# Local attention and a gated feed-forward layer on one core: scores of the first two blocks read straight from PSUM, and a new order of all operations

## The chip, the core and the metric

The kernel runs on one core of a Trainium2 chip. A core has five instruction queues: TensorE (PE in the profile, its weight loads PEld), VectorE (DVE), ScalarE (ACT), GpSimd (POOL) and SyncE (SP), which here issues all DMAs. Every queue executes its instructions in the order in which they stand, and waits for another engine through semaphores. TensorE writes into the eight banks of PSUM; the other engines read from there into SBUF. The metric is the device time of one execution in microseconds, the median of the runs.

## The reference, cut to what matters

```python
batch, heads, seq, D = 4, 8, 768, 64;  block, window = 32, 16;  nb = seq // block
k_sum = k.reshape(B, H, nb, block, D).max(axis=3)
v_sum = v.reshape(B, H, nb, block, D).mean(axis=3)
scores_l = scale * q @ k.T ;  mask_l = abs(i - j) < window
scores_s = scale * q @ k_sum.T + log(block)
scores_all = concat([where(mask_l, scores_l, -1e9), scores_s])
a = exp(scores_all - max(scores_all));  a = a / (sum(a) + 1e-9)
x = (a @ concat([v, v_sum])) as [3072 tokens, 512]
h = x @ w_in                       # 512 -> 2048
out = (h * cos(h)) @ w_out         # 2048 -> 512, all in float32
```

## The kernel before, in words

**Blocks and steps.** The 3072 tokens are cut into eight blocks of 384 (0 to 7, two for each of the four sequences). Attention of a block is done in four groups, one for each pair of heads, called a, b, c, d: `c0` is pair 2 of block 0. The feed-forward part is cut into 128 steps s0 to s127: a block by one of 16 slices of 128 of the 2048 hidden columns. Block 0 has s0 to s5 (hidden slices 0 to 5) and, after block 1's s6 to s21, its other ten, s22 to s31; the blocks from 2 on have 16 steps in a row. The weights of hidden slice f are w0 to w15.

**Attention of a group.** Keys and queries are loaded (L453) and turned by TensorE. The scores of a group stand in two PSUM banks, one for each head of the pair: 128 rows x 3 x 120 values each, that is 96 keys of the window and 24 block summaries for each half tile of 64 queries. For the groups of blocks 0 and 1 (the string `MASKS`) the mask is first put into the bank by TensorE: `place_masks` multiplies the identity by the float32 tile `mask` in two products, L556 for the window's columns and L559 for the summaries' columns, and `scores` (L569, L581) adds to it, with the queries already scaled. Then the two banks are copied to one SBUF tile of 128 x 6 x 120 (`scale`, which is a plain copy here, L366 on ScalarE or L368 on VectorE), VectorE takes the maximum of each row (L600), GpSimd subtracts it from the whole tile (`less_max`, L605), ScalarE takes the exponential of the whole tile in one instruction (L618), VectorE sums the rows (L621; a column of 1e-9 behind the 120 is summed too) and takes the reciprocal (L626), GpSimd multiplies by it (`normalize`, L629). TensorE turns the probabilities (`turn_p`, L638), they are copied to SBUF, and `values` (L682) multiplies them by the value rows; the result x is split into a high part `xh` and a low part `xl` (`rest`, L372). In the later blocks the scale and the mask go in with the copy from PSUM (L592).

**Values.** Value windows come by L474 and L482. The block means of the values come from their own loads, L897 for sequence 0 (products on TensorE, L905, in one bank of 512 columns) and L250 for the others, in eight pieces of 192 KB for each sequence, which GpSimd or VectorE add up (L255, L274). A piece can be loaded once its predecessor in the same buffer is added up, and the load waits for that on SP's queue. L489 spreads the means of sequence 0 to a group's value tile.

**A weight slice.** Two DMAs of about 511 KB (L387, L391) bring the packed weights; ScalarE takes them apart (`apart`, L400, `first_bits`, L406), VectorE joins the bits (`join`, L413), ScalarE or VectorE rounds to the high part (L366, L368), and VectorE or GpSimd forms the low part (`rest`, L372). Each of these is one instruction of 128 x 1024 for a slice.

**A step.** `up` (L726): 12 products of 384 columns over the four pairs c = 0 to 3, for each `wi_h` by `xh`, `wi_h` by `xl`, `wi_l` by `xh`. Then `turns` (L736, ScalarE), `residue` (L739, VectorE), `sine` (L744, ScalarE), `gate` (L748, VectorE), the high and low parts `gh` and `gl`, and the down products (L777) into three banks, which stay taken for a block's whole run: six with `gh` (`down`) and three with `gl` (`down_low`).

**What sets the order.** A hand-written string `ORDER` lists all operations of the program as words such as `a0.tk.1.0`: who (`a0` group, `s3` step, `w4` slice, `v1_2` piece 2 of sequence 1's value means), what (`l` load, `q` `k` `v` `m` loads of queries, keys, values and means, `tq` `tk` turns, `sc` scores, `z` scale, `mx` maximum, `su` less_max, `ex` exponential, `sm` sums, `iv` reciprocal, `nm` normalize, `tp` turn_p, `va` values, `xh` `xl` the parts of x, `up` `tu` `re` `si` `ga` `hi` `lo` `dh` `dl` the operations of a step), then PSUM banks or buffers as numbers, and the engine as a letter (a ScalarE, v VectorE, p GpSimd). The program is written out in that order, so each engine's queue has the order of its own words. A tile in SBUF that is reused, and a PSUM bank, makes its next writer wait for its last reader.

```python
MASKS = "11111111000000000000000000000000"
RUNS = ((0, 0, 6, "first"), (1, 0, 16, "whole"), (0, 6, 16, "last"))
```

Of the kernel before, what the change touches and what calls it, by code (L numbers as in the profile page):

```python
# [26 lines left out]
SLOTS = "6701676701267667"  # L27


ORDER = """  # L30
a0.k a0.tk.1.0 a0.ck.1.a a0.tk.0.1 a0.q a0.tq.2 a0.cq.a a0.ck.0.v c0.k c0.tk.1.7 a0.ks.0 c0.ck.1.v c0.q b0.k d0.k d0.q
c0.ks.1 a0.ks.1 w1.l a0.ms.1.2 c0.tq.3 c0.tk.0.4 c0.ks.0 a0.sc a0.z.0.v a0.z.1.a c0.ck.0.v b0.tk.0.0 b0.ck.0.a a0.mx
a0.su b0.ks.0 c0.cq.a d0.tk.0.7 b0.tk.1.6 b0.ck.1.v d0.ck.0.a c0.ms.5.1 d0.tk.1.2 c0.sc c0.z.1.v c0.z.0.a d0.ms.0.3
c0.mx c0.su b0.ks.1 d0.ks.0 b0.q b0.ms.4.5 b0.tq.1 b0.cq.v b0.sc d0.tq.1 w1.ab.1 a0.ex v0_0.l v0_0.vm.6 a0.v w1.sh
w1.fb b0.z.0.a d0.ks.1 c0.ex d0.cq.a c0.sm b0.z.1.v w1.hi.a w1.lo.p a0.sm d0.ck.1.a d0.sc d0.z.0.a c0.iv a0.iv b0.mx
b0.su c0.nm d0.z.1.a d0.mx v0_1.l v0_1.vm v0_1.ve.a c1.q a0.nm a0.tp.1.0 a0.tp.0.1 a0.cp.0.v w0.l w0.ab.1 w0.sh w0.fb
w0.hi.v w0.lo.v a1.q b1.q a0.cp.1.a a1.tq.7 a1.cq.a b1.tq.1 c1.tq.2 a1.ms.0.3 c0.tp.0.4 a1.sc w2.l d0.su b0.ex d0.ex
d0.sm b1.cq.v a1.z.0.a a1.z.1.a a0.m a0.va.5 c1.ms.0.1 c0.tp.1.3 d0.iv d0.nm d0.tp.1.6 a1.mx b0.sm w2.ab.1 c0.cp.0.a
w2.sh c0.cp.1.a a0.xh.a c1.cq.a w2.fb w2.hi.v b0.iv w2.lo.v c0.m c0.v c0.va.7 c0.xh.a d1.ms.2.3 c1.sc c1.z.0.v
c1.z.1.a a0.xl c0.xl b0.nm d0.tp.0.4 b1.ms.1.0 b0.tp.1.5 b1.sc b0.tp.0.7 w5.l w5.ab.1 w5.sh d0.cp.1.a d0.cp.0.a w5.fb  # L40
w5.hi.v b0.m d0.m w4.l d0.v d0.va.4 c1.mx d0.xh.v d0.xl w4.ab.0 d1.q d1.tq.6 b0.v b0.cp.1.a b0.cp.0.a b0.va.7 b0.xh.v
b0.xl a1.su d1.cq.a d1.sc b1.z.1.a a1.ex w4.sh b1.z.0.a w5.lo.p w4.fb w4.hi.v d1.z.0.a d1.z.1.a c1.su c1.ex a1.sm
d1.mx a1.iv w3.l w3.ab.1 w3.sh w3.fb s1.up.0 s0.up.1 s1.tu s0.tu w3.hi.a s2.up.2 w4.lo.p s4.up.3 a1.nm a1.tp.0.4
# [926 lines left out]
```

## Time and profile before

| what | value |
|---|---|
| median of 3 runs | 643.02 us (641.36 to 644.64) |
| profiled execution, its span | 640.1 us |
| TensorE busy | 621.7 us, 97% |
| VectorE busy | 428.5 us, 67% |
| ScalarE busy | 314.8 us, 49% |
| GpSimd busy | 212.2 us, 33% |
| read from and written to HBM | 53.69 MB, 15.73 MB |
| DMA queue of SP, share of 16 engines' span | 42.5% |
| chain of work that ended last | TensorE 88%, VectorE 3%, all others 2% or less |

The span is the profiled execution from its first to its last instruction, and the median lies 2.9 us above it; the profile gives no other time of that execution. Busy times are sums over the span. The chain is followed back from the last instruction, at each step to what released it. The grouped rows give busy time, mean duration of one in ns, the idle time of the engine just before them, and what ended most of that idle time. The rows of the timeline give start (us) and duration; `x6` at their end means that six instructions in a row are shown as one.

### The profile page before, as it was taken

The page shows a single profiled execution, that of the slowest core. Times are in us where ns is not written, and L with a number is a line of the kernel's source. Part 1 is how long each engine was busy: PE and PEld are TensorE (multiplying, and loading weights), DVE is VectorE, ACT ScalarE, POOL GpSimd, SP SyncE. Part 2 cuts the span into 40 slices and gives each one's busy share as a digit, 9 for nine tenths or more (in the row PEclk, how much of TensorE's full clock was granted, in tenths as well). Part 3 has the DMA queues.
Part 4 walks back from the last instruction along what each step waited for, and adds up shares of the span by engine and source line. Part 5 has one row for each costly group of instructions (what it writes and reads, how often), then busy time and mean ns, then how long its engine had stood idle before and what let it go on. Part 6 is the DMA issues. An engine that isn't in the chain of part 4 may idle for free.

```text
span 640.1 us, 12076 instructions
## 1 busy us (share of the span) xinstructions
PE 621.7 (97%) x4593; PEld 548.1 (86%) x4593; DVE 428.5 (67%) x787; ACT 314.8 (49%) x529; POOL 212.2 (33%) x236
## 2 busy tenths in 40 slices
PE   6789999999999999999999999999999999999997
PEld 6478898888888898898988988988888988989895
DVE  5688998878866687757767666566766566544334
ACT  2788765656543654345562634334443463522222
POOL 4556564144362433132543422213342131100101
PEclk9999999999999999999999999999999999999999
DMA  9998653642353447442335524522333421310001
GB/s 237 289 266 234 227 166 112 160 106 59 95 156 108 117 105 162 112 100 89 97 99 146 129 63 106 122 72 71 102 82 83 116 68 59 107 42 18 0 1 49
DMA packets 167569, 72.57 MB, mean 113 GB/s; under 512 B 134424, under 2 KB 156632, under 8 KB 167512
## 3 DMA queue, kind: packets, MB, share of 16 engines
q1 hardware_dynamic: 167368, 71.68, 42.5%
q8 instruction: 36, 0.59, 0.4%
q14 instruction: 21, 0.17, 0.1%
q10 hardware_dynamic: 144, 0.13, 0.1%
HBM read 53.69 MB, written 15.73 MB: 108 GB/s over the span
## 4 chain that ended last, share of the span: by engine, by line
PE 88%; DVE 3%; DMA 2%; ACT 2%; SPq 2%; POOL 1%; issue 1%; DVEq 0%; POOLq 0%; ACTq 0%
PE banks L777 41%; PE banks L726 39%; PE banks L682 4%; PE banks L569 3%; SPq L453 1%; DMA late<-in_moe_w_out_dram 1%; DMA late<-in_q_dram 1%; DVE stage L413 1%; PE banks L638 1%; DVE w L372 1%; ACT stage L400 1%; POOL late L629 0%; ACT first L406 0%; POOL w L372 0%; POOL sc L629 0%
## 5 line engine op out<-in xcount | busy, mean ns | idle before, releaser
L726 PE MATMUL banks<-xh,w 128*128 128x384 f32 x1024 | 269.0, 337 | 2.1 <-DVE t L748 1.4
L777 PE MATMUL banks<-w,gh 128*128 128x512 f32 x768 | 197.8, 392 | 0.0
L726 PEld LDWEIGHTS banks<-xh,w 128*128 128x128 f32 x1024 | 185.4, 188 | 6.0 <-DVE t L748 2.0
L726 PE MATMUL banks<-xl,w 128*128 128x384 f32 x512 | 171.2, 334 | 0.0
L777 PEld LDWEIGHTS banks<-w,gh 128*128 128x128 f32 x768 | 142.5, 188 | 30.9 <-DVE gh L368 1.3
L372 POOL TENSOR_TENSOR gl<-t,gh 128x384 fp32r<-128x384 f32 x63 | 66.5, 1057 | 261.3 <-DVE gh L368 144.2
L736 ACT ACTIVATE t<-banks 128x384 int32<-128x384 f32 x128 | 61.9, 489 | 132.9 <-PE banks L726 58.7
L739 DVE SCALAR_TENSOR_TENSOR t<-t,banks 128x384 f32<-128x384 int32 x128 | 69.1, 545 | 67.2 <-ACT t L736 66.4
L777 PE MATMUL banks<-w,gl 128*128 128x512 f32 x384 | 109.3, 392 | 0.0
L744 ACT ACTIVATE t<-t 128x384 f32<-128x384 f32 x128 | 66.0, 523 | 72.8 <-DVE t L739 72.5
L726 PEld LDWEIGHTS banks<-xl,w 128*128 128x128 f32 x512 | 96.1, 188 | 0.4
L748 DVE TENSOR_TENSOR t<-t,banks 128x384 f32<-128x384 f32 x128 | 69.5, 547 | 34.1 <-ACT t L744 33.4
L777 PEld LDWEIGHTS banks<-w,gl 128*128 128x128 f32 x384 | 71.4, 188 | 16.0 <-POOL gl L372 0.8
L629 POOL TENSOR_TENSOR sc<-sc,r 128x720 f32<-128x720 f32 x28 | 39.9, 1425 | 53.0 <-DVE r L626 49.3
L605 POOL TENSOR_TENSOR sc<-sc,m 128x720 f32<-128x720 f32 x28 | 39.7, 1419 | 53.6 <-DVE m L600 53.6
L366 ACT CAST gh<-t 128x384 fp32r<-128x384 f32 x58 | 29.4, 510 | 40.9 <-DVE t L748 22.1
L372 DVE TENSOR_TENSOR gl<-t,gh 128x384 fp32r<-128x384 f32 x65 | 37.6, 581 | 11.3 <-ACT gh L366 5.4
L368 DVE CAST gh<-t 128x384 fp32r<-128x384 f32 x70 | 27.9, 399 | 17.3 <-PE banks L777 14.1
L621 DVE TENSOR_REDUCE r<-sc 128x6 f32<-128x726 f32 x28 | 25.2, 900 | 14.4 <-ACT sc L618 14.3
L592 DVE SCALAR_TENSOR_TENSOR sc<-banks,mask 128x360 f32<-128x360 f32 x48 | 24.2, 522 | 13.9 <-PE banks L569 13.7
L618 ACT ACTIVATE sc<-sc 128x720 f32<-128x720 f32 x28 | 22.6, 807 | 21.4 <-POOL sc L605 21.3
L255 POOL TENSOR_TENSOR kn<-kn 96x256 f32<-96x256 f32 (+1 forms) x32 | 22.8, 712 | 25.8 <-DMA kn<-in_v_dram 17.9
(109 smaller groups left out, 573.4 us busy)
## 6 DMA issues: line engine op xcount, KB each, us to landing
pd<-stage SPq DMA_DIRECT2D x22, 384.0 KB
late<-in_moe_w_out_dram SPq DMA_DIRECT2D x16, 511.6 KB
late<-in_moe_w_in_dram SPq DMA_DIRECT2D x16, 510.5 KB
pt<-pd SPq DMA_DIRECT2D x66, 96.0 KB
vn<-in_v_dram SPq DMA_DIRECT2D x50, 120.0 KB
...
kn<-in_v_dram SPq DMA_DIRECT2D x24, 192.0 KB
...
```

The lines of the kernel that those rows point to most:

```text
L366: eng.copy(out=out, in_=in_)
L368: eng.tensor_copy(out=out, in_=in_)
L372: eng.tensor_tensor(out=lo, in0=src, in1=hi.bitcast(F32), op=ALU.subtract)
L605: nc.gpsimd.tensor_tensor(out=self.sc, in0=self.sc, in1=self.m.unsqueeze(2).broadcast_to([P, U, NK]), op=ALU.subtract)
L629: nc.gpsimd.tensor_tensor(out=self.sc, in0=self.sc, in1=self.r.unsqueeze(2).broadcast_to([P, U, NK]), op=ALU.mult)
L682: nc.tensor.matmul(out=self.xps[rows, t * QT : (t + 1) * QT], lhsT=self.vn[:, t, rows], rhs=self.pt[2 * c + hh][s], start=True, stop=True,)
L726: nc.tensor.matmul(out=self.h, lhsT=w_of(name, self.f)[:, c * P : (c + 1) * P], rhs=x_of(self.blk, part, c), start=n == 0, stop=n == last,)
L736: nc.scalar.activation(out=self.t.bitcast(I32), in_=self.h, func=AF.Copy, scale=1.0 / TWO_PI, bias=0.25)
L739: nc.vector.scalar_tensor_tensor(out=self.t, in0=self.t.bitcast(I32), scalar=-TWO_PI, in1=self.h, op0=ALU.mult, op1=ALU.add)
L744: nc.scalar.activation(out=self.t, in_=self.t, func=AF.Sin, scale=-1.0, bias=-0.5 * math.pi)
L748: nc.vector.tensor_tensor(out=self.t, in0=self.t, in1=self.h, op=ALU.mult)
L777: nc.tensor.matmul(out=self.acc[i], lhsT=g[:, i * P : (i + 1) * P], rhs=w_of(name, self.f), start=self.first and n == 0, stop=self.last an ...
```

## The change

Four things change, most of them in the first 90 us or so of the program.

1. **Mask by one product.** For blocks 0 and 1 `place_masks` makes one bfloat16 product of 128 x 360 for each bank, from two small tiles `pick` and `apart` that stand in the tile `early` and are made by some twenty selections on GpSimd at the start. (A product of zeros and ones with a table of mask rows; the logarithm of 32 is summed from three bfloat16 numbers.)
2. **Maximum and exponential from PSUM.** For these eight groups the queries are scaled by -SCALE, so the banks hold negated scores. There is no copy; the maximum is two VectorE reductions (one for each bank, `min`), `less_max` and `sums` are gone, and the exponential is six ScalarE instructions of 128 x 120 for each group, which read PSUM, add the maximum as a bias and give the row sum in an accumulator. VectorE adds 1e-9 to the sums ahead of the reciprocal. A score bank is now held until its three exponentials are done.
3. **Up products by head pair.** `up_chunk` (word `u`) issues the three products of one pair; block 0's s0 to s5 use it, with the pairs in the order 0, 2, 3, 1 and the chunks of s0, s1 and s2 mixed.
4. **Buffers and order.** The tiles of a step's gate, the maxima, sums and value means have explicit numbers in place of an automatic rotation; a slice is told at its load which raw tile it takes; the means of sequence 0 stand in `early` and are made in two groups of partitions (24 products of 256 columns in place of 12 of 512). `ORDER` is new in its first 860 words or so, up to about s40 and d3; behind that the words stand as before, apart from the numbers of buffers and banks.

The core of the diff:

```diff
         def place_masks(self, *two):
             self.score_banks(two)
-            where = mask[:, self.half : self.half + QC, :]
             for sp in self.sp:
                 nc.tensor.matmul(
-                    out=sp[:, :, :W], lhsT=upper(ident), rhs=upper(where[:, :, :W]), start=True, stop=False
-                )
-                nc.tensor.matmul(out=sp[:, :, W:], lhsT=ident, rhs=where[:, :, W:], start=False, stop=False)
+                    out=sp, lhsT=pick.rearrange("p h q -> p (h q)"), rhs=apart[:, self.half : self.half + QC, :],
+                    start=True, stop=False,
+                )
...
-        def scale(self, hh, eng):
-            out = self.sc.rearrange("p (c h) n -> p c h n", h=2)[:, :, hh, :]
-            if self.masks:
-                copy(eng, out, self.sp[hh])
...
+        def maximum(self, i):
+            m = self.m = ms[i]
+            if not self.masks:
+                nc.vector.tensor_reduce(out=m, in_=self.sc, axis=AX.X, op=ALU.max)
                 return
...
-        def maximum(self):
-            m = self.m = att.tile([P, U], F32, name="m", bufs=2)
-            nc.vector.tensor_reduce(
-                out=m, in_=self.sc, axis=AX.X, op=ALU.min if self.fused else ALU.max
-            )
+            for hh in range(2):
+                nc.vector.tensor_reduce(
+                    out=m.rearrange("p (c h) -> p c h", h=2)[:, :, hh], in_=self.sp[hh], axis=AX.X, op=ALU.min
+                )
...
+        def exp(self, i):
+            self.r = rs[i]
+            if not self.masks:
+                nc.scalar.activation(out=self.sc, in_=self.sc, func=AF.Exp)
+                return
+            for hh in range(2):
+                for c in range(QC):
+                    u = 2 * c + hh
                     nc.scalar.activation(
-                        out=self.sc[:, u, :], in_=self.sc[:, u, :], func=AF.Exp, bias=self.m[:, u : u + 1],
+                        out=self.sc[:, u, :], in_=self.sp[hh][:, c, :], func=AF.Exp, bias=self.m[:, u : u + 1],
                         scale=-1.0, accum_out=self.r[:, u : u + 1],
                     )
-            else:
-                nc.scalar.activation(out=self.sc, in_=self.sc, func=AF.Exp)
...
         def inverse(self):
-            if self.fused:
+            if self.masks:
                 nc.vector.tensor_scalar_add(self.r, self.r, 1e-9)
             nc.vector.reciprocal(out=self.r, in_=self.r)
...
+        def up_chunk(self, c, *i):
+            if i:
+                self.h, self.n = bank(*i)[:, :TB], 0
+            for name, part in (("wi_h", 0), ("wi_h", 1), ("wi_l", 0)):
+                nc.tensor.matmul(
+                    out=self.h, lhsT=w_of(name, self.f)[:, c * P : (c + 1) * P], rhs=x_of(self.blk, part, c),
+                    start=self.n == 0, stop=self.n == 3 * NC - 1,
+                )
+                self.n += 1
```

(In the kernel before, `fused` is false for every group, so its branches are not taken.)

The new order at three places. First SP's queue, which issues the DMAs. Before, behind the loads of sequence 0's keys and slices w1, w0, w2, w5, w4, it goes on with d1's queries (`qn`), values and means and the slices w3 (`late_125`) and w8 (`late_124`):

```order
L453 DMA qn<-in_q_dram 128x3x64 x2
L474 DMA early<-in_v_dram 96x5x64 x2
L482 DMA early<-in_v_dram 80x2x64
L387 DMA late_125<-in_moe_w_in_dram 128x4x1021
L391 DMA late_125<-in_moe_w_out_dram 128x4093
L489 DMA late_128<-late_128 24x6x128
L489 DMA late_127<-late_126 24x6x128
L387 DMA late_124<-in_moe_w_in_dram 128x4x1021
L391 DMA late_124<-in_moe_w_out_dram 128x4093
```

Now the pieces of sequence 1's value means (`kn`) stand between the slices w5 (`late_128`) and w4 (`late_122`):

```order
L245 DMA kn<-in_v_dram 96x512
L523 DMA x_1_197<-early 24x6x128
L424 DMA late_128<-in_moe_w_in_dram 128x4x1021
L428 DMA late_128<-in_moe_w_out_dram 128x4093
L523 DMA early<-early 24x6x128
L245 DMA kn<-in_v_dram 96x512
L508 DMA early<-in_v_dram 96x5x64 x2
L516 DMA early<-in_v_dram 80x2x64
L424 DMA late_122<-in_moe_w_in_dram 128x4x1021
L428 DMA late_122<-in_moe_w_out_dram 128x4093
L245 DMA kn<-in_v_dram 96x512
```

Eight of these pieces, all issued behind w3 before, now stand ahead of or around w5, w4 and w3, and each waits on this queue until its buffer has been added up.

Second, ScalarE near the start, with the first groups' work between the parts of the first slice (`stage` and `first` are the tiles of `apart` and `first_bits`). Before, copies from the score banks (`128x3x120`) and one exponential a group (`128x6x120`):

```order
L400 ACTIVATE stage_324<-late_131 128x1024
L618 ACTIVATE sc<-sc 128x6x120
L406 ACTIVATE first<-stage_324 128x1024
L366 COPY sc<-banks 128x3x120
L618 ACTIVATE late_129<-late_129 128x6x120
L510 ACTIVATE late_126<-banks 128x384
L366 CAST w_345<-stage_324 128x1024
L366 COPY kd_102<-banks 128x384
L366 COPY late_129<-banks 128x3x120 x2
```

Now six exponentials a group, straight from the banks:

```order
L442 ACTIVATE first<-stage_260 128x1024
L544 ACTIVATE qd<-banks 128x384
L544 ACTIVATE late_123<-banks 128x384
L649 ACTIVATE sc,r_83<-banks,m_81 128x120 x6
L436 ACTIVATE stage_360<-late_128 128x1024
L649 ACTIVATE sc,r_84<-banks,m_82 128x120 x6
L442 ACTIVATE first<-stage_360 128x1024
L544 ACTIVATE late_123<-banks 128x384
L649 ACTIVATE late_126,r_83<-banks,m_81 128x120 x6
```

The bits of the first slice now come ahead of the first exponential, and the score copies are gone.

Third, TensorE around the first down products (L777 before, L819 now; the prediction calls the first of them the mark). Before, the last up product of s3 (`w_741` is w3), then transposes and values of block 1's groups and the down products of s0 (`w_410` is w0) and s1 (`w_345` is w1):

```order
L726 MATMUL banks<-xh_0_527,w_741 128x384
L638 MATMUL banks<-ident,late_129 120x128 x2
L682 MATMUL banks<-pt,late_127 64x64 x12
L777 MATMUL banks<-w_410,gh 128x512 x6
L777 MATMUL banks<-w_410,gl 128x512 x3
L638 MATMUL banks<-ident,late_129 120x128 x4
L777 MATMUL banks<-w_345,gh 128x512 x6
```

Now (`w_892` is w4, `w_522` w0, `w_294` w1), the up products by pair of s4 stand around them, and s3's come later:

```order
L771 MATMUL banks<-xl_0_743,w_892 128x384
L771 MATMUL banks<-xh_0_741,w_892 128x384 x2
L771 MATMUL banks<-xl_0_743,w_892 128x384
L771 MATMUL banks<-xh_0_741,w_892 128x384
L716 MATMUL banks<-pt,late_125 64x64 x12
L819 MATMUL banks<-w_522,gh_77 128x512 x6
L771 MATMUL banks<-xh_0_641,w_892 128x384
L771 MATMUL banks<-xl_0_669,w_892 128x384
L771 MATMUL banks<-xh_0_641,w_892 128x384
L819 MATMUL banks<-w_294,gl_80 128x512 x3
L819 MATMUL banks<-w_294,gh_78 128x512 x6
```

What stood ahead of the mark as s3's up products now is most of s4's, the turns of block 1's first groups have moved ahead of it, and a down step starts with its low part where that is there first.

More of the change, by code (lines that the diff above doesn't have):

```diff
@@ new lines, in tile_kernel, with keep, below @@
+    TURN = 16
+    EDGES = LAST + 1 + 3 * TURN
+    SECOND = (EDGES + P) // 2
+    def keep(t, pattern, op, base, mult, fill):
+        nc.gpsimd.affine_select(
+            out=t, in_=t, pattern=pattern, compare_op=op, fill=fill, base=base, channel_multiplier=mult
+        )
+    def below(t, rows, fill):
+        keep(t, [[0, n] for n in t.shape[1:]], ALU.is_ge, rows - 1, -1, fill)
+    nc.gpsimd.memset(pick, 0.0)
+    for d in range(3):
+        keep(pick, [[0, 2], [1, QT]], ALU.not_equal, d, -1, 1.0)
@@ new lines, in tile_kernel @@
+    for i, one in enumerate(logs):
+        below(far, LAST + 1 + i * TURN, -one / TURN)
+    below(far, EDGES, 0.0)
+    mask = const.tile([P, QC + 1, NK], F32, name="mask")
+    nc.vector.memset(mask[:, :, 0:W], 0.0)
+    nc.vector.memset(mask[:, :, W:NK], -LOGB)
+    for hh in range(2):
+        rows = mask[hh * QT : (hh + 1) * QT, :, 0:W]
+        nc.gpsimd.affine_select(
+            out=rows, in_=rows, pattern=[[0, QC + 1], [1, W]], compare_op=ALU.is_ge,
+            fill=-NEG, base=-1, channel_multiplier=-1,
+        )
+        nc.gpsimd.affine_select(
+            out=rows, in_=rows, pattern=[[0, QC + 1], [-1, W]], compare_op=ALU.is_ge,
+            fill=-NEG, base=2 * WINDOW - 1, channel_multiplier=1,
+        )
@@ L341, in w_of @@
+    nc.vector.memset(mask[:QT, 0, :WINDOW], -NEG)
+    nc.vector.memset(mask[QT:, QC, W - WINDOW : W], -NEG)
     def w_of(name, f):
@@ L759, in down @@
             if self.first:
-                accs[:] = [bank(i) for i in banks]
-            self.acc = list(accs)
+                accs[self.run] = [bank(i) for i in banks]
             self.products(self.early())
@@ L806, in take @@
             if self.kind == "first":
-                copy(eng, self.o[i], self.acc[i])
+                copy(eng, self.o[i], accs[self.run][i])
             else:
-                self.negative(eng, self.o[i], self.acc[i])
+                self.negative(eng, self.o[i], accs[self.run][i])
         def negative(self, eng, to, from_):
@@ L862, in tile_kernel @@
     vn_b = [carve(late[3 + i // 2], i % 2 * n_v, NK, U, P) for i in range(NG)]
-    means = [carve(late[2 + i], 2 * n_v + TB, NB, P) for i in range(NG)]
-    slices = [Slice(f, late[int(i)][:, :RAW]) for f, i in enumerate(SLOTS)]
+    all_means = carve(early, 1280, NB, H * D)
+    means = [all_means[:, i * P : (i + 1) * P] for i in range(NG)]
+    slices = [Slice(f) for f in range(NF)]
     for t in sc[2:]:
```

408 lines of the change are left out of this document (213 added, 195 removed).

## The prediction

> **What bounds the kernel now.** I read the page first, then the busy times by stretch, then TensorE's waits, then its timeline around the first products of the feed-forward part.
>
> ```profile
> span 640.1 us, 12076 instructions
> ```
>
> ```profile
> 0.00:10.00 10.00, 5.32 (x24) 4.65 (x24) 4.05 (x10) 2.25 (x3) 5.41 (x37) 1.00 0.88 200
> 10.00:20.00 10.00, 8.27 (x183) 7.04 (x183) 7.04 (x12) 6.07 (x10) 2.78 (x2) 1.00 1.00 281
> 20.00:30.00 10.00, 7.39 (x71) 3.08 (x70) 5.78 (x11) 6.47 (x15) 7.80 (x5) 1.00 1.05 318
> 30.00:40.00 10.00, 8.55 (x183) 7.40 (x183) 9.36 (x14) 7.14 (x14) 2.87 (x2) 1.00 1.05 284
> 40.00:50.00 10.00, 9.03 (x177) 8.06 (x176) 8.20 (x13) 9.20 (x16) 6.04 (x5) 1.00 0.96 237
> 50.00:60.00 10.00, 8.79 (x52) 7.96 (x50) 8.65 (x13) 8.42 (x11) 7.72 (x5) 1.00 0.87 214
> 60.00:640.00 580.00, 574.39 (x3915) 509.95 (x3913) 385.37 (x720) 275.29 (x466) 179.61 (x183) 1.00 0.37 99
> ```
>
> The columns behind the stretch are TensorE, its weight loads, VectorE, ScalarE and GpSimd (busy us and count), then granted clock, DMA share and GB/s. From 60 us on TensorE is idle for 580 - 574.4 = 5.6 us in all, and most of that is the store at the end. In the first 60 us it is idle for 60 - 47.4 = 12.6 us, while the DMA share stands near 1. So there is nothing to win behind 60 us except by giving TensorE less to do, and at most some 10 us ahead of it. What TensorE waits for there:
>
> ```profile
> PE banks L517 <- POOL mask L293: 4.6, 1, 4.6
> PE banks L638 <- POOL sc L629: 2.5, 2, 2.2
> PE banks L638 <- POOL late L629: 1.5, 2, 1.0
> ```
>
> The first row is the start, before any key has landed. The next two are transposes of the probabilities behind GpSimd's normalizing. The change touches this head, so I compare two kernels at one mark, the first down product of s0, and ask when each gets there and what TensorE has behind it by then.
>
> ```profile
> 12.46 0.34 PE L559 MATMUL banks<-mask,ident 128*128 128x72 f32 x2
> 12.64 0.29 PE L556 MATMUL banks<-mask,ident 128*128 128x288 bf16 x1
> 12.77 0.34 PE L559 MATMUL banks<-mask,ident 128*128 128x72 f32 x2
> 46.82 0.44 PE L726 MATMUL banks<-xh,w 128*128 128x384 f32 x1
> 60.90 1.65 PE L777 MATMUL banks<-w,gh 128*128 128x512 f32 x6
> 63.09 0.60 PE L638 MATMUL banks<-ident,late 128*120 128x128 f32 x4
> 63.44 1.64 PE L777 MATMUL banks<-w,gh 128*128 128x512 f32 x6
> 66.15 0.92 PE L682 MATMUL banks<-pt,late 120*64 120x64 f32 x24
> 67.00 0.43 PE L638 MATMUL banks<-ident,late 128*120 128x128 f32 x2
> ```
>
> The mark is at 60.90 before. A step's up product first runs at 46.82.
>
> **The change, part by part.**
>
> Masks. A bank costs 0.31 us before (12.46 to 12.77). 288 bf16 columns take 0.13 of that (12.64 to 12.77), so 360 take about 0.16; below by the 0.13 itself, above by 0.31. 16 banks x 0.15 = 2.3 us of TensorE (0 to 2.8). All of it lies ahead of the mark, where TensorE waits anyhow, so it is not added to the sum: it is inside the time of the mark.
>
> Maximum, exponential, row sums. The rows of the first 60.9 us:
>
> ```profile
> L605 POOL TENSOR_TENSOR sc<-sc,m 128x720 f32<-128x720 f32 x4 | 5.6, 1388 | 6.8 <-DVE m L600 6.8
> L621 DVE TENSOR_REDUCE r<-sc 128x6 f32<-128x726 f32 x3 | 2.7, 901 | 0.0
> L600 DVE TENSOR_REDUCE m<-late 128x6 f32<-128x720 f32 x4 | 3.6, 899 | 0.4 <-ACT late L366 0.3
> L618 ACT ACTIVATE late<-late 128x720 f32<-128x720 f32 x4 | 3.3, 818 | 0.0
> L366 ACT COPY sc<-banks 128x360 f32<-128x360 f32 x6 | 2.7, 464 | 5.5 <-PE banks L581 5.5
> L368 DVE COPY sc<-banks 128x360 f32<-128x360 f32 x2 | 1.1, 528 | 0.7 <-PE banks L581 0.7
> L618 ACT ACT_TABLE_LOAD x1 | 1.3, 1283 | 0.0
> 23.35 0.82 ACT L366 COPY late<-banks 128x360 f32<-128x360 f32 x2 [1.44 <-PE banks L581]
> 26.04 0.73 ACT L366 COPY late<-banks 24x128 f32<-24x128 f32 x4 [1.86 <-PE banks L905]
> ```
>
> Eight subtractions leave GpSimd (8 x 1.39 = 11.1 us), eight row sums leave VectorE (7.2), four copies too (2.1); the eight maxima become 16 halves of some 0.5 us each (a copy of the same 360 values takes 0.53), 8.4 in place of 7.2, with eight small additions more. ScalarE loses 12 copies and eight exponentials (12 x 0.46 + 8 x 0.82 = 12.1 busy) and gets 48 exponentials of 120 values with a bias column and a row sum. No such instruction is in the trace. From below, four 24x128 copies run 0.16 apart ((0.73 - 0.25)/3); from above, 360-value copies run 0.36 apart (0.82 - 0.46). I take 0.25, nearer to the first in size but with two operands more: 12.0 us (7.7 to 17.3). One switch of ScalarE's table ahead of the mark goes as well (1.28), since all exponentials now stand ahead of the first sine. So ScalarE comes out even, VectorE and GpSimd lose work, and a pair's way from scores to normalized weights is shorter by a copy, the subtraction and the sum (0.5 + 1.4 + 0.9) less 0.7 for the six exponentials (6 x 0.25 - 0.82): 2.1 us. The price: a score bank is held until its exponentials are done, and four banks' reuse (c0's query transposes in bank 4 behind a0's exponentials) waits for it.
>
> The Trainium skill ("ScalarE: Activation LUTs", section "What ACT_TABLE_LOAD costs") gives an activation with a pointer bias 280 ns + 0.833 ns per element with 93 ns overlap, an estimate of 0.29 us at 120 elements, and no price for the row sum. It speaks against this part: six small instructions pay the fixed part six times. By it ScalarE would have 1.8 us more than I take, and the time would be about 639.5 us; the sum below goes by 0.25.
>
> The new order. Loads first: four keys and slice w1 now precede the queries, so the first scores come near 15 us in place of 10; later five of the eight 192 KB pieces of batch 1's value summaries stand ahead of slice w4 on SP's queue, and SP waits for GpSimd's sums between them. Behind the first scores the up products of s0, s1, s2 start with pair 0, whose x needs no other pair.
>
> ```profile
> late<-in_moe_w_out_dram SPq DMA_DIRECT2D x16, 511.6 KB
> late<-in_moe_w_in_dram SPq DMA_DIRECT2D x16, 510.5 KB
> kn<-in_v_dram SPq DMA_DIRECT2D x24, 192.0 KB
> SPq L250 <- POOL vs L274: 16.2, 4, 6.9
> L413 DVE SCALAR_TENSOR_TENSOR stage<-late,first 128x1024 int32<-128x1024 int32 x6 | 8.5, 1416 | 4.6 <-ACT first L406 3.5 <-POOL w L372 1.1
> L406 ACT ACTIVATE first<-stage 128x1024 int8<-128x1024 f32 x6 | 8.2, 1371 | 0.1
> L372 POOL TENSOR_TENSOR w<-stage,w 128x1024 fp32r<-128x1024 f32 x3 | 7.2, 2385 | 8.0 <-ACT w L366 4.1 <-DVE w L368 4.0
> L400 ACT ACTIVATE stage<-late 128x1024 f32<-128x1024 int8 x6 | 6.9, 1147 | 2.1 <-DMA late<-in_moe_w_out_dram 2.1
> L368 DVE CAST w<-stage 128x1024 fp32r<-128x1024 f32 x4 | 2.8, 694 | 0.1
> 80.82 14.58 PE banks L726 x84
> ```
>
> When is the mark reached? On TensorE's queue the mark stands behind the first eight and a last product of s4, and these need w4. Ahead of and with w4, SP's queue holds five slices (5 x 1022 KB), five v pieces (960), all keys and queries of batch 0 (3072), its values twice (1536 and 1120 for four pairs) and four means (288): 12086 KB or 12.4 MB. The stretches move 10.8 MB by 40 us and 2.4 in the next ten, so w4 lands near 46.5; with SP's waits for the v sums I take 48. Then L400, L406, L413, the cast and GpSimd's low part: 1.1 + 1.4 + 1.4 + 0.7 + 2.4 = 7.0, so 55, plus 1.5 for ScalarE's and VectorE's queues in front of them; seven products of s4 behind it (7 x 14.58/84 = 1.2) and one value product (0.85): 58.6, with hops between engines 59. That is 1.9 us ahead of 60.9. If the queues cost nothing it is 57, if each of the three long ones waits for a landing it is 63.
>
> What lies behind TensorE at the mark: the new order has put 16 transposes (16 x 0.35/4 = 1.4) and two value products (2 x 0.85) of block 1 ahead of it and leaves three up products (0.5) and nothing else behind that was ahead; three query transposes of d1 (0.4) are ahead too. So 3.0 us less is left to do.
>
> Sum: (60.9 - 59.0) + 3.0 = 4.9 us. Behind the mark TensorE has next to no waits to lose, so a new order there can only add some; I put 0.4 for that. 4.5 us off. The profiled execution's span of 640.1 becomes 635.6; with the 2.9 us that the median of the runs (643.0) has over this span, 638.5 us.
>
> Costed at nothing: the longer setup on GpSimd (some 20 small selections, about 5 us beside 5.4 busy) hides behind the loads up to 14 us; the block-0 value means' split in two banks hides in TensorE's waits near 25 us; were that cover gone, each would cost its own microseconds once.
>
> **The rivals.** First, slower: weight slices too late. w3 is the sixth slice, behind 14.4 MB; by the stretches it lands near 55.7, its low part is ready near 63 to 65, and TensorE wants it (s3's up) 5.5 us behind the mark, at 64.5. There is no slack, and SP's longest single wait for a GpSimd sum before was 6.9 us. One such wait ahead of w4 and one ahead of w3 would take the mark to 66 and hold s3 further: 4.5 - 6.9 - 3 = 5 us slower, 648. It decides once w4 lands after 54. For it: the row of SP's waits. Against: GpSimd has lost 11 us of subtractions ahead of these sums. Second, no change: an exponential costs 0.36 us on ScalarE. 48 x 0.11 = 5.3 us more in the queue that makes each slice's bits, of which waits absorb about 2: mark at 62, time 641.5. Third, the head is hidden anyway: VectorE, 0.86 to 0.94 busy there, sets the mark at 60.9 as before, and only the 3.0 us of moved work show: 640.0.
>
> **How the numbers follow.** A measurement of this kernel tells some 0.5% (3.2 us) from no change, as three runs lie 3.3 us apart. The forecast (mark at 55 to 60, 634.5 to 639.8) has 0.58; the second and third rival, with a mark between 60.5 and 63, 0.27 together, nearly all inside 0.5%; the late slices 0.15, half of it over 0.5% slower by far. The range reaches from the mark at 55 without late waits, 633.5, to the rival of late slices' milder half, 645.5. So faster 0.59, same 0.27, slower 0.14.
>
> **What would show it.** First scores near 15 to 16 us; the first up product near 40; the mark near 59; exponentials 0.25 us apart; s3's up without a wait before it; TensorE idle in the first 60 us still above 8 us, and at most 6 behind. Wrong if SP waits for v sums ahead of w4 or w3 stretch to 5 us and more, if new idle behind 80 us exceeds 3 us, or if ScalarE is busy without a break ahead of the mark.

## The result, and the profile after

The changed kernel takes 650.5 us where the kernel before takes 643.0: a ratio of 1.0104 (1.0069 to 1.0139). One of its five executions took 1556 us, with TensorE's products of 384 columns at 679 ns in place of 337; the ratio leaves it out (the other four have a median of 649.5), and since it was the profiled one, the rows below are from a second set's profiled execution (span 650.0 us). That second set gave 650.4 against 643.7, 1.0100 (1.0071 to 1.0130). It is slower by 1%, where 0.7% faster was forecast; the time lies above the range.

The medians are 6.7 to 7.5 us apart and the two profiled spans 9.9 (650.0 and 640.1). So 2 to 3 us of the differences between the two profiles are scatter of single executions.

First the same stretches as before (TensorE, its weight loads, VectorE, ScalarE, GpSimd, then granted clock, DMA share, GB/s):

```profile
0.00:10.00 10.00, 2.05 (x8) 1.34 (x9) 3.18 (x9) 1.28 (x1) 9.11 (x52) 1.00 0.85 197
10.00:20.00 10.00, 7.59 (x39) 5.72 (x41) 6.76 (x13) 4.32 (x7) 0.83 (x5) 1.00 0.97 282
20.00:30.00 10.00, 7.21 (x212) 5.55 (x204) 5.82 (x12) 7.85 (x34) 1.39 (x1) 1.00 0.76 225
30.00:40.00 10.00, 8.97 (x215) 6.86 (x208) 7.37 (x18) 9.14 (x38) 7.64 (x8) 1.00 0.77 210
40.00:50.00 10.00, 8.28 (x129) 6.65 (x130) 8.20 (x16) 8.33 (x31) 8.68 (x12) 1.00 0.60 181
50.00:60.00 10.00, 7.83 (x59) 7.38 (x59) 5.86 (x11) 6.34 (x18) 4.75 (x3) 0.83 0.83 228
```

From 20 to 50 us the DMA share is 0.60 to 0.77, where it was 0.96 to 1.05, and VectorE has lost work. No engine is busy throughout; ScalarE, with 0.79 to 0.91, comes nearest. TensorE's timeline (start, duration) at the first scores, the first up product, its longest wait behind the first scores, and the mark, and then GpSimd's low part of w4:

```profile
19.62 1.86 PE L614 MATMUL banks<-kd,qd 64*64 64x96 f32 x48
...
47.47 0.45 PE L771 MATMUL banks<-xh,w 128*128 128x384 f32 x1
...
54.36 0.92 PE L716 MATMUL banks<-pt,early 120*64 120x64 f32 x24 [2.17 <-issue]
...
69.02 1.66 PE L819 MATMUL banks<-w,gh 128*128 128x512 f32 x6
```

```profile
64.04 2.37 POOL L409 TENSOR_TENSOR w<-stage,w 128x1024 fp32r<-128x1024 f32 x1 [5.00 <-DVE w L405]
```

The mark comes at 69.0 us, 8.1 behind that of before. The nine products of s4 ahead of it start at 66.4, when w4's low part is ready (64.04 + 2.37). But TensorE had no long wait for it: from 55.2 us to the mark it is idle for 0.4 us. Up to the mark it is idle for 18.5 us, against 12.7 before; of these 5.8 us more, 3.9 fall in the first 20 us and 1.9 behind them. Behind the mark 650.0 - 69.0 = 581.0 us are left, against 640.1 - 60.9 = 579.2. So 8.1 of the 9.9 us between the two spans are lost ahead of the mark and 1.8 behind it.

SP's queue (issue times of the w_in half of w2, w5, w4 and w3 with pieces `kn` between them, then SP's waits up to 62 us: sum, count, longest):

```profile
28.97 0.37 SPq L424 DMA_DIRECT2D late<-in_moe_w_in_dram  x1
...
42.47 0.33 SPq L245 DMA_DIRECT2D kn<-in_v_dram  x1
44.38 0.46 SPq L424 DMA_DIRECT2D late<-in_moe_w_in_dram  x1
49.42 0.35 SPq L245 DMA_DIRECT2D kn<-in_v_dram  x1
51.41 0.39 SPq L424 DMA_DIRECT2D late<-in_moe_w_in_dram  x1
...
61.11 0.53 SPq L424 DMA_DIRECT2D late<-in_moe_w_in_dram  x1
```

```profile
SPq L245 <- POOL vs L271: 3.4, 1, 3.4
SPq L245 <- DVE vs L260: 2.9, 2, 1.9
SPq L940 <- DVE stage L449: 2.5, 1, 2.5
SPq L523 <- ACT early L403: 2.0, 1, 2.0
SPq L424 <- PE banks L949: 1.7, 1, 1.7
SPq L245 <- POOL vs L269: 1.3, 1, 1.3
```

Before, the same four slices went out at 23.3, 30.5, 33.5 and 42.2 us:

```profile
23.32 1.68 SPq L387 DMA_DIRECT2D late<-in_moe_w_in_dram  x1
30.50 0.39 SPq L387 DMA_DIRECT2D late<-in_moe_w_in_dram  x1
33.45 0.51 SPq L387 DMA_DIRECT2D late<-in_moe_w_in_dram  x1
42.20 0.39 SPq L387 DMA_DIRECT2D late<-in_moe_w_in_dram  x1
```

They are 5.7, 13.9, 18.0 and 18.9 us later now. SP stands 7.6 us (3.4 + 2.9 + 1.3) for sums of the pieces and 6.2 (2.5 + 2.0 + 1.7) for other engines' work.

The chain of work that ended last shows the same (start, duration; some of its links). It goes from a piece's load to its sum, from there to SP's next load, and on to a slice:

```profile
42.47 2.83 DMA kn<-in_v_dram
45.44 1.60 POOL kn L250
...
49.42 2.96 DMA kn<-in_v_dram
52.41 1.03 DVE vs L260
53.45 6.40 DMA kn<-in_v_dram
...
61.11 0.53 SPq L424
...
64.27 7.08 DMA late<-in_moe_w_out_dram
...
74.02 3.83 DMA kn<-in_v_dram
```

In the kernel before, the chain stands on TensorE from the mark on:

```profile
60.97 2.28 PE banks L777 x9
```

ScalarE's row of `apart` (L436) for w4 starts at 59.40, the exponentials of one group at 22.15, 22.50, 22.84:

```profile
22.15 0.36 ACT L649 ACTIVATE sc<-banks,m 128x120 f32<-128x120 f32 x1 [3.80 <-DVE m L632]
22.41 0.19 ACT L649 ACTIVATION_READ_ACCUMULATOR sc<-banks,m 128x1 f32 x1
22.50 0.35 ACT L649 ACTIVATE sc<-banks,m 128x120 f32<-128x120 f32 x1
...
22.84 0.36 ACT L649 ACTIVATE sc<-banks,m 128x120 f32<-128x120 f32 x1
...
59.40 1.14 ACT L436 ACTIVATE stage<-late 128x1024 f32<-128x1024 int8 x1 [2.84 <-issue]
```

### The profile page after: what moved, and what is told of

Read it like the earlier page. It is cut to its first block, busy times and chain, and to the rows that moved or that the text cites. A ratio compares the mean times of both kernels' runs of the same rounds, so it can differ in the third digit from the quotient of the medians.

```text
span 1554.5 us, 12127 instructions
## 1 busy us (share of the span) xinstructions
PE 1541.1 (99%) x4573; PEld 1053.1 (68%) x4573; DVE 419.2 (27%) x784; ACT 330.4 (21%) x612; POOL 195.9 (13%) x241
## 3 DMA queue, kind: packets, MB, share of 16 engines
q1 hardware_dynamic: 167368, 71.68, 17.2%
## 4 chain that ended last, share of the span: by engine, by line
PE 99%; DVE 0%; SPq 0%; DMA 0%; issue 0%; ACT 0%; DVEq 0%
PE banks L819 44%; PE banks L759 42%; PE banks L716 4%; PE banks L602 3%; PE banks L771 2%; PE banks L672 1%; PE banks L614 1%; PE banks L949 0%; PE banks L589 0%; PE banks L551 0%; PE banks L538 0%; SPq L487 0%; DMA x<-in_k_dram 0%; DVE kd L570 0%; DVE kd L405 0%
## 5 line engine op out<-in xcount | busy, mean ns | idle before, releaser
L759 PE MATMUL banks<-xh,w 128*128 128x384 f32 x976 | 566.5, 679 | 0.0
L819 PE MATMUL banks<-w,gh 128*128 128x512 f32 x768 | 484.5, 828 | 0.0
L759 PEld LDWEIGHTS banks<-xh,w 128*128 128x128 f32 x976 | 350.5, 361 | 94.4 <-issue 85.2
L819 PEld LDWEIGHTS banks<-w,gh 128*128 128x128 f32 x768 | 266.5, 348 | 179.0 <-issue 174.4
L759 PE MATMUL banks<-xl,w 128*128 128x384 f32 x488 | 332.7, 682 | 0.0
L819 PE MATMUL banks<-w,gl 128*128 128x512 f32 x384 | 258.5, 829 | 0.0
L759 PEld LDWEIGHTS banks<-xl,w 128*128 128x128 f32 x488 | 161.5, 331 | 51.9 <-issue 48.4
L819 PEld LDWEIGHTS banks<-w,gl 128*128 128x128 f32 x384 | 133.1, 348 | 88.9 <-issue 86.3
L716 PE MATMUL banks<-pt,vn 120*64 120x64 f32 x600 | 48.8, 372 | 0.0
L602 PE MATMUL banks<-first,qd 64*64 64x120 f32 x576 | 42.6, 482 | 0.0
```

Of the source, the lines that this page charges most:

```text
L602: nc.tensor.matmul(out=self.sp[hh][s * QT : (s + 1) * QT, c, :], lhsT=self.qd[rows, t * QT : (t + 1) * QT], rhs=self.kw[rows, t, :], start ...
L716: nc.tensor.matmul(out=self.xps[rows, t * QT : (t + 1) * QT], lhsT=self.vn[:, t, rows], rhs=self.pt[2 * c + hh][s], start=True, stop=True,)
L759: nc.tensor.matmul(out=self.h, lhsT=w_of(name, self.f)[:, c * P : (c + 1) * P], rhs=x_of(self.blk, part, c), start=n == 0, stop=n == last,)
L819: nc.tensor.matmul(out=accs[self.run][i], lhsT=g[:, i * P : (i + 1) * P], rhs=w_of(name, self.f), start=self.first and n == 0, stop=self.l ...
```

## The experiments

Marks are those of one profiled execution, and they scatter: two executions of nearly the same kernel had 60.9 and 66.4 (before, and before_warm below). In the second the granted clock was 0.71 from 20 to 30 us and 0.84 from 50 to 60, in the first 1.00 throughout. So verdicts rest on ratios to the kernel before, and marks only show the place.

**The changed kernel again** gave the rows above.

> The changed kernel once more, unedited, since its profiled execution is one in which every product of TensorE took twice its time (384 columns in 0.68 us in place of 0.34) from the first to the last, while the other four runs had a mean granted clock of 0.987 to 0.996 (before: 1.00). Theory 1 (TensorE's clock): the kernel itself is quicker by a few us, but its first 20 us leave TensorE gaps, so its products go on at half speed far behind 11 us, where those of the kernel before reach full speed; a trace shows 128-column turns and score products at twice their time until 20 us or later, the granted clock's row below 1.00 in some stretch of the first 60 us, and the span is 643.5 us plus half the time that is run at half speed. Theory 2 (late weights): products run at full speed from about 12 us on, and the mark (first L819) comes at 64 us or later behind a wait for w4's low part, with SP waiting 5 us and more for a GpSimd sum ahead of w4 or w3.

Score products are at half speed until about 21 us, as theory 1 there said (48 of them take 1.86 us at 19.62 and 1.09 at 24.91), and granted clock is down to 0.83 from 50 to 60 us. The mark comes behind 64 us, as theory 2 said, but TensorE has no long wait for w4, and SP's longest wait for a sum is 3.4 us and not 5. Neither theory is borne out whole. So I named three causes: late slices, ScalarE's exponentials, TensorE's clock.

**Slices ahead.**

```diff
-... v0_1.l w0.ab.0 ... w2.l.0 a0.m ... a0.v ... w5.l.7 ... w4.l.1 ... w3.l.6 ... w8.l.0
+... v0_1.l w2.l.6 w0.ab.0 ... w5.l.7 a0.m ... a0.v w4.l.1 ... c0.v w3.l.0 ... w2.fb w8.l.6
```

> The changed kernel with five words of the order moved: w2, w5, w4, w3 and w8 are loaded ahead of the pieces of sequence 1's value means that stood before them (w2 into a raw tile that is free from the start). Nothing else is edited. Theory 1 (the prediction's first rival: slices too late, because SP's queue stands behind GpSimd's sums): w4's bits begin before 48 us (59.4 now), the mark comes at 59 to 62 us (69.0 now), and the time is 641 to 644 us. Theory 2 (ScalarE: 48 exponentials that start 0.34 us apart, 16 us in a queue that runs without a break from 22 to 48 us): the slices land earlier but wait in ScalarE's and VectorE's queues, the mark comes only 1 to 3 us earlier, 647.5 to 649.5 us. Theory 3 (TensorE at half speed until 20.6 us, and once more near 55 us, is what costs the time): within 1.5 us of 650.4.

649.7 us, 1.0089 (1.0066 to 1.0112): nothing that differs from the changed kernel. The mark stays (69.9), the rest behind it is shorter (647.2 - 69.9 = 577.3 us). From TensorE's waits, and ScalarE's row of `apart` for w4:

```profile
PE banks L716 <- DMA x<-in_v_dram: 3.1, 1, 3.1
60.05 1.19 ACT L436 ACTIVATE stage<-late 128x1024 f32<-128x1024 int8 x1
```

Now TensorE waits for c0's values, which stand behind the slices on SP's queue. SP issues w4 at 34.7 us in place of 51.4, and ScalarE still takes it apart at 60.05 (59.40 in the changed kernel), since ScalarE takes its queue in order and has waited there for 2.4 us for TensorE (at 49.4) by then. Theory 1 in this form falls: earlier slices alone don't bring the mark forward.

**Two exponentials a group.**

```diff
             for hh in range(2):
-                for c in range(QC):
-                    u = 2 * c + hh
-                    nc.scalar.activation(
...
+                nc.scalar.activation(
+                    out=self.sc.rearrange("p (c h) n -> p c h n", h=2)[:, :, hh, :], in_=self.sp[hh], func=AF.Exp,
+                    bias=self.m[:, hh : hh + 1], scale=-1.0, accum_out=self.r[:, hh : hh + 1],
+                )
```

> The changed kernel, but each group of blocks 0 and 1 has two exponentials of 128 x 360 (one for each bank) in place of six of 128 x 120; a bank's three half tiles share one bias column and one row sum, so the weights are normalized with the wrong maxima and sums. Only the count and shape of ScalarE's instructions differ: 16 that start some 0.55 us apart (9 us) in place of 48 at 0.34 (16 us). Theory 2 (ScalarE's queue): the mark comes 4 to 7 us earlier, 643.5 to 646.5 us. Theory 1 (SP's queue behind GpSimd's sums and other waits): SP's waits shrink a little with it, the mark 1 to 3 us earlier, 647.5 to 649.5 us. Theory 3: within 1.5 us of 650.4.

647.6 us, 1.0056 (1.0040 to 1.0073): 2.8 us less than the changed kernel, with the mark at 65.5. In this order ScalarE takes part.

**New operations, old order** (words of `ORDER` against those of the kernel before).

```diff
-a0.sc a0.z.0.v a0.z.1.a ... a0.mx a0.su ... a0.ex ... a0.sm
+a0.sc a0.mx.0 a0.ex.0 ...
```

> The code of the changed kernel (one mask product a bank, maximum and exponential from PSUM) under the order of the kernel before: all words as there, but the maximum and the exponential of blocks 0 and 1 stand where the second of the two copies stood, and copies, subtractions and row sums are gone; up products whole, not by pair. Theory 1 (the new order's loads are the fault, the new operations are not): 639 to 643 us, at or below the 643.7 of the kernel before. Theory 2 (the operations themselves cost it, through ScalarE): 646 to 650 us. Theory 3 (TensorE's clock suffers because four products a group's mask, now two, kept it busy early): score products at half speed beyond 14 us, and 644 to 648 us.

685.5 us, 1.0642 (1.0624 to 1.0660), far from all three. TensorE's waits up to 80 us:

```profile
PE banks L588 <- ACT late L648: 3.3, 2, 2.1
...
PE banks L588 <- ACT sc L648: 2.8, 2, 2.3
```

Mask products (L588) wait for ScalarE's exponentials: the banks are held, and the old order reuses them at once. The mark is at 79.05, and 682.8 - 79.05 = 603.8 us follow; why the rest is longer too I did not follow up. So the new operations, set into the old order in this way, cost far more than the whole change. The old operations in the new order were not run, so what the order costs without them is not known.

**TensorE kept warm.**

```diff
-d0.k a0.k b0.k c0.k a0.tk.0.0 b0.tk.1.2 w1.l.1 ... b0.tk.0.3 c0.q
+warm.10 d0.k a0.k b0.k c0.k a0.tk.0.0 warm.2 b0.tk.1.2 warm.4 w1.l.1 ... b0.tk.0.3 warm.6 c0.q
...
+                zero = first.bitcast(BF16)
+                for _ in range(int(what)):
+                    nc.tensor.matmul(out=bank(4), lhsT=zero[:, :P], rhs=zero[:, :512], start=True, stop=True)
```

> The changed kernel with 22 more products of TensorE, 128 x 512 of zeros in bfloat16 into bank 4 which nothing reads: ten ahead of the first key turn and twelve among the key turns, where TensorE waits for keys and VectorE. Theory 3 (the clock): 128-column turns and scores are at full speed from about 10 us on (20.6 us now), the first scores start 1.5 us earlier, and the time falls by 2 to 4 us, 646.5 to 648.5. Theories 1 and 2: the head waits for loads and ScalarE anyhow, 649.5 to 651.

651.8 us, 1.0111 (1.0064 to 1.0158). The first scores start at 17.2 in place of 19.6 us, and the median gains nothing, so the half speed of the first 20 us does not explain the loss.

The granted clock later on is another matter, and no run here holds it. Its mean over an execution was 0.992 in the changed kernel's ten other executions and 0.995 in the nine of the kernel before in the second set. From that 0.3% of 650 us, an estimate, it can be up to 2 of the 6.7 us. In this run the one execution at 0.998 took 646.6 us, and the three at 0.984 to 0.992 took 651.8 to 654.0. Whether a lower clock lengthens the head, or a head with more waits lowers the clock, is not shown.

**The same in the kernel before** (bank 6, ten products).

> The kernel before with ten more products of TensorE ahead of its first key turn (128 x 512 zeros in bfloat16 into bank 6, which nothing reads until 19.6 us). If TensorE's half speed in the first 11 us sits on the path, the first scores come 1 to 2 us earlier than 10.07, the mark 1 to 2 us earlier than 60.9 and the time is 641.5 to 642.5 us; if loads and VectorE set the mark there, the first scores come earlier and the time stays within 0.7 us of 643.4.

642.7 us, 0.9987 (0.9973 to 1.0001): first scores at 9.4 for 10.1 us, and no difference clear of noise. Its profiled execution was its longest (span 645.7 us, mark at 66.35): the head of one kernel varies by 5 us.

**All three edits together, and slices moved less far.**

> The changed kernel with the three edits of before together: five slices loaded earlier, two exponentials a group in place of six (weights normalized with wrong maxima and sums), 22 products of zeros early on. If the three causes are separate, their effects on the profiled executions add: the mark 3.5 us earlier by the exponentials and 3.2 by the clock than 69.0, the stretch behind it 3.6 us shorter by the loads, which gives 639.5 to 642 us. If one wait stands behind all of them (values that land late because slices stand ahead of them), the mark stays at 66 us and more, and the time at 645 to 648.

> The changed kernel, complete, with the products of zeros early on and the slices moved less far than in the run with slices ahead: w2 and w5 as there, but w4 behind d0's values, w3 behind b0's and w8 behind w3. If the values that landed late there ate what the slices won, the first up product comes at 44 to 46 us (52.7 there, 47.5 in the changed kernel), the mark at 62 to 64 us, and the time is 643.5 to 646 us; if ScalarE's 48 exponentials set the mark whatever the loads do, it stays at 66 us and the time at 647 to 650.

649.3 us, 1.0087 (1.0065 to 1.0110), and 650.4 us, 1.0112 (1.0087 to 1.0136). The effects don't add, and both marks are past 70 us. In the first TensorE waits 4.3 us for c0's values. Whichever loads I put first, others were late. From this I guessed that something takes DMA time or SP's time that isn't there to take.

**No pieces of sequence 1's value means.**

```diff
-... v1_0.l ... v1_0.s.0.v ... v1_7.l ... v1_7.s.p ...
...
+    for hg in range(2):
+        vsum[1, hg] = vss[hg][0][: HG * NB]
+        nc.vector.memset(vsum[1, hg], 0.0)
```

> The changed kernel without the eight pieces of sequence 1's value means: neither their loads nor their sums are done, the means are zeros (so the summaries of that sequence's values are left out of its blocks). Nothing else moves. Theory 1 (SP's queue, which stands behind the pieces' sums and carries their 1.5 MB ahead of the slices): SP issues w5, w4 and w3 5 to 9 us earlier than 44.4, 51.4 and 61.1, the mark comes at 61 to 64 us and the time is 641 to 645 us. Theory 2 (ScalarE's exponentials) gives the mark at 67 to 69 and 648 to 650.

642.0 us, 0.9978 (0.9958 to 0.9999): 8.4 us less than the changed kernel, the largest gain of all.

```profile
40.00:50.00 10.00, 9.04 (x132) 7.68 (x133) 7.25 (x16) 9.08 (x33) 3.60 (x3) 1.00 0.92 260
50.00:60.00 10.00, 9.72 (x116) 8.35 (x114) 7.39 (x12) 9.27 (x23) 4.83 (x3) 1.00 0.84 230
...
63.64 0.50 PE L821 MATMUL banks<-w,gh 128*128 128x512 f32 x1
```

The mark stands at 63.6 us, and 639.9 - 63.6 = 576.3 us follow. TensorE's idle time from 40 to 60 us falls from 3.9 to 1.2 us. SP issues w5, w4 and w3 at 40.6, 44.3 and 54.2 us, 3.8 to 7.1 earlier than the changed kernel and still 10 to 12 later than the kernel before. So the pieces make about a third of the slices' delay; the rest comes with other parts of the change, which no run takes apart. This run leaves out the pieces' work, and not only their place.

**Is it their sums, their bytes or their place on SP's queue?** One kernel loads the pieces without adding them up, one issues the loads from GpSimd's queue:

```diff
-            nc.sync.dma_start(out=t[:, c : c + step], in_=flat[:, i * cols + c : i * cols + c + step])
+            (nc.gpsimd if b == 1 else nc.sync).dma_start(
+                out=t[:, c : c + step], in_=flat[:, i * cols + c : i * cols + c + step]
+            )
```

> The changed kernel with the eight pieces loaded as they are but not added up (the means of sequence 1's values are zeros). SP waits for a piece's predecessor to land, no longer for a sum. If SP's waits for sums or GpSimd's and VectorE's time in them cost the 8.4 us, 641.5 to 645 us; if the 1.5 MB ahead of the slices do, 647 to 650 us.

> The changed kernel, complete, with the eight loads of sequence 1's value pieces issued from GpSimd's queue in place of SP's, at the same places of the order; GpSimd adds most of them up itself. Loads, sums and bytes stay, only SP's queue no longer stands behind the sums. If these waits are what makes the slices late, most of the 8.4 us that the run without the pieces won comes back: mark 62 to 65 us, time 641.5 to 645 us. If the 1.5 MB themselves or GpSimd's time for the sums do it, the mark stays at 67 us or later and the time at 647 to 651.

Without sums 645.7 us, 1.0025 (1.0011 to 1.0040): of the 8.4 us, 4.7 are the sums (SP's waits for them and the time of GpSimd and VectorE), 3.7 the loads and SP's waits for them to land; by the ratios it is 4.8 and 3.0. From GpSimd's queue 653.0 us, 1.0149 (1.0122 to 1.0175), above what either theory there had, with the mark at 71.5. SP then issues w5, w4 and w3 at 40.1, 43.9 and 54.6, as early as without pieces, and the wait reappears on GpSimd (its timeline, and TensorE's wait for it):

```profile
43.71 0.54 POOL L245 DMA_DIRECT2D kn<-in_v_dram  x1
50.01 1.27 POOL L252 TENSOR_TENSOR kn<-kn 96x256 f32<-96x256 f32 x2 [5.76 <-DMA kn<-in_v_dram]
...
54.36 1.40 POOL L665 TENSOR_TENSOR late<-late,r 128x720 f32<-128x720 f32 x1
...
PE banks L674 <- POOL late L665: 4.4, 2, 3.4
```

GpSimd stands 5.8 us for the piece to land, a normalization stands behind it, and TensorE's transposes wait for that.

**Values ahead**, since weights_ahead had made them late.

```diff
+... a1.q a0.v ... c1.q c0.v d0.v w2.l.6 ... a0.m w5.l.7 ... c0.m b0.v ... d0.m w4.l.1 ... b0.m w3.l.0
```

> The changed kernel, complete, with the loads in the order in which TensorE needs them: the values of block 0 (c0, d0, a0, b0) go out ahead of w2 and of SP's wait for the means, w2 next into the free raw tile, w5, w4, w3 behind the means of a0, d0 and b0, pieces of sequence 1's means behind these where they can be. If the 12.1 MB ahead of the mark and the time that SP leaves the DMA engines idle set the mark, the DMA share of 25 to 50 us rises from 0.53-0.81 to 0.85 and more, no value tile is waited for over 1 us, the mark comes at 61 to 64 us, and the time is 641.5 to 645 us. If ScalarE's 48 exponentials do, the mark stays behind 66 us and the time at 647 to 650.

> The same order of loads with two exponentials a group in place of six (wrong maxima and sums, as before). If both the loads and ScalarE take part, this is 2 to 4 us below the run with the order of loads alone; if the loads alone set the mark, within 1 us of it.

653.4 us, 1.0152 (1.0106 to 1.0197), and with two exponentials 655.6, 1.0180 (1.0132 to 1.0227). The marks come at 73.8 and 76.1, and the two exponentials won nothing here: the second is 2.2 us above the first, where 2 to 4 below or no difference was expected (the intervals overlap). In the first the DMA share rises to 0.98 from 20 to 30 us and 0.93 from 30 to 40, and falls to 0.49 from 40 to 50 us, at a granted clock of 0.68. SP now stands behind the pieces' landing (up to 80 us):

```profile
SPq L246 <- DMA kn<-in_v_dram: 8.7, 3, 5.7
```

**Two exponentials without pieces.**

> The changed kernel without the pieces of sequence 1's means (zeros) and with two exponentials a group in place of six (wrong maxima and sums). With the pieces gone the mark stood at 63.6 us, 4.6 us behind the 59 of the prediction. If ScalarE's exponentials (0.34 us apart where 0.25 was taken) make up most of that, the mark comes at 59 to 61 us and the time at 638 to 640.5 us; if late first scores (19 us where 15 to 16 was taken) and the half clock do, it stays at 62 us or later, and the time within 1.5 us of 642.0.

642.1 us, 0.9975 (0.9959 to 0.9992), as without pieces alone. So the 2.8 us of the exponentials are no cost of their own: they showed with the pieces in the changed kernel's order, and neither without the pieces nor in the order with values ahead. What makes the difference is not shown.

**The pieces past 100 us**, complete kernels: first right behind the turns of block 2's keys, then behind the last slice, each also with the warm products.

```diff
-... v1_0.l ... v1_7.s.p ... a2.k ... d2.kt.0 ... w14.l.6 ...
pieces_late:
+... d2.kt.0 v1_0.l ... w14.l.6 ... v1_7.s.v ...
pieces_late2:
+... d2.kt.0 ... w14.l.6 s15.ga v1_0.l ... v1_7.s.p ... v2_0.l ...
```

> The changed kernel, complete, with the eight pieces of sequence 1's value means (and the first four of sequence 2's) moved out of the head: they come behind the turns of block 2's keys, past 100 us, where the DMA share is about 0.35 and SP has no slice left to load. If the pieces' place in the head is what made the changed kernel slower, the head becomes that of the run without pieces (mark 62 to 65 us) and the time 640.5 to 643.5 us, with at most 1.5 us given back by new waits behind 100 us. If the run without pieces was fast because the pieces' work was left out, 645 us or more.

> The same with the 22 products of zeros among the first key turns. In the run without pieces TensorE waited only 0.5 us between 40 us and the mark, so an earlier start should now count: the first scores start near 17.2 in place of 18.9 us, and the time is 1 to 2 us below pieces_late, about 639.5 to 642 us, and below the kernel before's 643.5. If the head waits for loads again, within 0.7 us of pieces_late.

> The changed kernel, complete, with the pieces moved out of the head as in pieces_late, but behind the last weight slice (w14), one every sixteen words, and added up by GpSimd alone, so that no slice stands behind a piece on SP's queue and VectorE waits for none. In pieces_late the head was as fast as without pieces (mark 64.1 us) and 16 us of TensorE's time went in waits between 115 and 160 us, for slices that stood behind pieces and for scores whose copies stood behind sums. If these waits are gone, mark 63 to 65, idle behind the mark 1.5 to 4 us and time 641 to 645 us; if block 2's own work cannot do without the early pieces, idle behind the mark 8 us or more and time above 650.

> The same with the 22 products of zeros among the first key turns: 1 to 2 us below pieces_late2 if the late first scores are on the path once the pieces are gone, and then 639.5 to 643 us; within 0.7 us of it if not.

663.6 us, 1.0306 (1.0276 to 1.0336); 661.2, 1.0275 (1.0240 to 1.0310); 650.8, 1.0115 (1.0095 to 1.0134); 649.4, 1.0090 (1.0067 to 1.0113). The head is that of the run without pieces in each, with marks from 63.1 to 64.2. TensorE's longest waits behind the mark (two of pieces_late, one of pieces_late2):

```profile
PE banks L603 <- ACT t L788: 5.1, 1, 5.1
PE banks L760 <- POOL w L410: 4.4, 1, 4.4
```

```profile
PE banks L819 <- POOL gl L409: 3.1, 1, 3.1
```

What the head won is given back: 661.9 - 64.1 = 597.8 and 649.2 - 64.2 = 585.0 us follow the mark. In the first, a slice's low part (L410) stands on GpSimd behind a piece's sum, which waits 3.5 us for its piece to land; in the second, a step's low part stands there behind a sum that waits 2.8 us. The warm products go with 2.3 and 1.4 us less here, with intervals that overlap. Both kernels come out where the second theory put them (645 us or more, and above 650 with 8 us or more of idle time behind the mark, where it is 10.9). None of the ten edited versions of the changed kernel that keep all its work beats the kernel before.

## Why the prediction was wrong

The step that failed is the arrival of w4: SP's waits were to move it from 46.5 to 48 us, and ScalarE began its bits at 59.4, where 49.5 was left room for (48 and 1.5 for the queues in front). ScalarE is idle for 2.8 us ahead of that; the profile does not name what it waited for. The steps behind it were right. From these bits to the low part it took 7.0 us (59.40 to 66.41), as in the prediction, and the products from there to the mark took 2.6 (66.39 to 69.02), where 2.05 was taken. So the steps of the path were the predicted ones, and its first term was 9.9 us too small. The path was not the only one: TensorE reached the nine products just then, so in this trace its own late start ends at the same moment, and which of the two would hold the mark alone is not shown.

Two parts of that term were wrong. The bytes were right: the queue ahead of and with w4 is 12086 KB, and SP had issued them by 52.4 us. But the rate was taken from the stretches of before, where the DMA share was near 1; here it was 0.60 to 0.77 for 30 us. And the 1.5 us for SP's waits, all for sums, were 6.6 us of sums by 51.4 us, when w4 is issued (3.4 + 1.9 + 1.3), with 6.2 more for other engines' work, for which the prediction had no term.

This comes nearest to the first rival (late slices, 648 us), by its own condition, w4 after 54; it had 0.15. The row that speaks for it (6.9 us of one wait) was quoted, and was set aside since GpSimd loses subtractions. But SP waits in order, and the rows of its waits name VectorE, ScalarE and TensorE beside GpSimd. The rival is not the whole cause either: with w4 issued 17 us earlier the time stayed (649.7 us), since ScalarE took it apart as late as before.

Point by point:

- Masks: four products take the 0.70 us from 36.44 to 37.14, 0.18 each; 0.16 was taken, inside the range.

```profile
36.44 0.77 PE L589 MATMUL banks<-early 128*128 128x360 bf16 x4
37.14 1.07 PE L614 MATMUL banks<-kd,qd 64*64 64x96 f32 x47
```

- Exponentials: 0.34 us apart (22.15 to 22.50 to 22.84), 48 of them 16.3 us, where 0.25 and 12.0 were taken; near the upper end of 0.36. The Trainium skill's page "ScalarE: Activation LUTs" (section "What ACT_TABLE_LOAD costs") gave an estimate of 0.29, nearer than mine; the read of the row sum, which it doesn't price, has rows of its own here. The size was wrong by 4.3 us. Two exponentials a group save more of ScalarE's time than that and won between 2.8 us and nothing.
- The maximum: 0.53 us a half, as taken.

```profile
L632 DVE TENSOR_REDUCE m<-banks 128x3 f32<-128x360 f32 x16 | 7.5, 525 | 3.0 <-PE banks L614 3.0
```

- First scores near 15 to 16: 19.6. The keys of four groups stand ahead of all queries, and TensorE is at half speed to 21 us in place of 11 (before, 48 score products take 1.30 us at 10.07 and 1.09 at 13.36). Warm products brought 2.4 us of it back and no time in the median.
- First up product near 40: 47.5. Mark at 59: 69.0.
- 3.0 us less work behind the mark: right in the run without pieces, where TensorE is busy for 570.4 us there, against 573.5 before; in the changed kernel it is 571.6. The 0.4 us for new waits there is a mis-sized term: TensorE is idle for 9.4 us behind the mark, against 5.7 before, which makes 3.7.
- The sum: 10.0 us at the mark and 4.4 behind it are the 14.4 between the predicted span of 635.6 and 650.0. By the medians the miss is 12.0 (638.5 against 650.5).
- The third rival (VectorE sets the mark) is out: VectorE has 0.58 to 0.82 of 20 to 50 us.
- The signs: TensorE is idle for 18.1 us in the first 60, above the 8 named, and for 9.8 behind them, where at most 6 was named. SP's longest wait for a sum was 3.4 us, under the 5 named as a sign of being wrong; it was the number of waits that counted.

What the runs show: leaving the pieces out of the head wins 1.2% (1.0100 against 0.9978), some 4.7 us by their sums and 3.7 by their loads. Not shown: that one queue's waits alone do it, since on GpSimd's queue they cost as much; that their place and not their work is the cost, since the two complete kernels that move them lose the gain elsewhere; and how much of the loss is granted clock. That without the pieces the mark is still at 63.6 and not 59 was not settled; two exponentials move it to 62.5, with no effect on the time. And even without the pieces, which the kernel before does carry, this change is worth 0.2%.
